# mLSTM attention with a feed-forward layer on one core: the later gates as 128 rows of chunk, sequence and head, and more bfloat16 products into tiles that are overwritten

## The chip, the core and the metric

The kernel runs on one core of a Trainium2 chip. The metric is device time in microseconds (us). A core has TensorE (PE, with its weight loads as PEld), VectorE (DVE), ScalarE (ACT), GpSimd (POOL) and SyncE (SP), which issues most of the DMAs here. Each engine carries out its instructions in the order of its own queue. An instruction that waits holds up everything behind it on its engine, and on no other.

## What is computed

Four sequences of eight heads have 768 tokens with 40 channels each. A gated recurrence (mLSTM) runs over the tokens, and its output is the input of a feed-forward layer with 2048 hidden units:

```
m_new = maximum(f_gate[t] + m, i_gate[t])
f_stab, i_stab = exp(f_gate[t] + m - m_new), exp(i_gate[t] - m_new)
C = f_stab * C + i_stab * outer(v[t], k[t])
n = f_stab * n + i_stab * k[t]
y[t] = sigmoid(o_gate[t]) * (C @ q[t]) / maximum(abs(n @ q[t]), 1)
...
h = x @ w_in                       # x: y as 3072 tokens of 320 channels
out = (maximum(h, 0) + alpha * minimum(h, 0)) @ w_out
```

## The kernel before

**Chunks.** Each sequence is cut into six chunks of 128 tokens, 24 in all. Inside a chunk the recurrence is an attention: scores pS = K Q, multiplied by a decay E = exp(L[t] + b[s]) that is zero for s > t, then times the values (pH). What came before the chunk enters through a state C, which `update` carries from chunk to chunk. L is the running sum, within a chunk, of lf = f + m(t-1) - m(t); b is i - m - L; the weights w = exp(b + L at the chunk's end), e = exp(L) and gam = exp(L at the chunk's end) scale the keys, the part from the state, and the state. The engines need b, w and e by token, as columns of bT, wT, eT, so they are transposed on PE. Two chunks make a group of 256 tokens; there are twelve groups, and the feed-forward layer runs group by group (`up`, `down`, lines 576 to 635) while the attention of the next group runs beside it.

**The gates.** They are kept as 32 rows (4 sequences x 8 heads, `BH`) of 768 tokens. `scan` (line 969) makes m for all tokens. Chunks 0 and 1 (columns `t0`) go first: lf0a, lf0b, li0, L0, bj0. Chunks 2 to 5 (columns `t1`, 512 of them) follow on POOL: lf1a and lf1b (lines 972 and 975), li1 (line 1037), then the running sum L1 on DVE (line 978), bj1 on POOL (line 1040), and after the written order `weights` (line 848), three Exp on ACT (lines 1099 to 1105), and twelve transposes of 32x128 by `by_token` (line 856). For chunks 2 and 3 L is spread over the partitions by a product with `pick` (line 412): LP holds three bfloat16 parts of L as 96 rows, so that one product adds all three. From chunk 4 on, L is read back from DRAM (`L_d`, written at line 1057) by a broadcast load Lb (line 113).

**The order.** The first group, up to its input x of the feed-forward layer, is written out as the string `ORDER` (line 559), and `pin` fixes it on every engine. Names in it: `dq0` and so on are DMAs on SP; `sp` spreads L, `ex` is the Exp of E, `ms` the mask of E on POOL (line 905), `sc` the scores, `wg` the product of both on DVE (line 925), `v0` and `v1` the values, `wd` the weighted keys kd (line 139), `w0s` to `w2l` the conversion of the first weights of the feed-forward layer, `x0` and `x1` the transposes of x (line 462). `warm12` is twelve bfloat16 products of the identity into a tile `junk` that nobody reads (line 942). After this string a scheduler lays out the rest; each engine takes it in that layout's order.

**Loads.** DMAs take eight semaphores in turn, over SP's and ACT's queues together, and each waits until the one before it on its semaphore has landed. SP's pinned order begins with f, q and k of chunks 0 and 1, weights, v, more weights (line 678) and the output gates `og` (line 122); the gates f and i come in by one load each (lines 817 and 818).

**After the string.** `weights(GC, NC)`, the conversion of two further weight blocks (w[3:]), the gates by token, gam, and `update(1)`; then FF0 and FF1 (the first two groups of the layer) with conversion of the other weights on ACT (lines 688, 710) and DVE (lines 700, 702, 714) beside the attention of chunks 2 to 5. From group 2 on the weights are there.

## Time and profile before

| | before |
|---|---|
| runs | 497.86, 503.60 and 499.66 us; median 499.66 us |
| the profiled execution | 500.96 us, its span 499.2 us |
| busy | PE 477.7 us (96%), DVE 321.6 (64%), ACT 321.6 (64%), POOL 304.8 (61%) |
| granted TensorE clock | 0.99 over the span |
| DMA | 61.60 MB |

The span is what the profiler's records cover; 1.76 us of the execution's time lie around it. Times in views are counted from the span's start. A row of the timeline has the start, the duration, the engine, the line, the operation with its tiles and its shape; in brackets at its end stands how long the engine idled before it, and what ended that. A row of the windows has a stretch, its length, the busy time of each engine in it, the granted clock and the share of time in which the 16 DMA engines had packets.

### The profile page before, as it was taken

To read this page: it belongs to the slowest core of one execution; us is meant where nothing else is said; L and a number is where in the kernel's file an instruction comes from. 1 tells how busy PE (TensorE), PEld (TensorE's weight loads), DVE (VectorE), ACT (ScalarE), POOL (GpSimd) and SP (SyncE) were. 2 spreads that over 40 slices of the span, in tenths; PEclk is the share of its full clock that TensorE was granted. 3 is DMA by queue.
4 is the path that set the end of the run, shared out by engine and by line. 5 is a ranking of instruction groups with operands and counts; after the bars stand their busy time and mean duration, and the time that the engine had idled before them with its cause. 6 is when DMAs were issued, how large, how long until landed. Compare 5 with 4: busy or idle time off the path is not lost.

```text
span 499.2 us, 11801 instructions
## 1 busy us (share of the span) xinstructions
PE 477.7 (96%) x4463; PEld 457.2 (92%) x4463; DVE 321.6 (64%) x676; ACT 321.6 (64%) x700; POOL 304.8 (61%) x393
## 2 busy tenths in 40 slices
PE   8889889989999999999899999999999999999997
PEld 7778879989989999989799999989999999999997
DVE  6889999934577686764395686567586575642321
ACT  3869697656587677756976677677886673343332
POOL 6632262306469889839498789858878755243242
PEclk9989997999999999999999999999999999999999
DMA  9999976345676566597557575769663130000000
GB/s 169 228 189 278 229 203 183 82 79 125 145 181 146 92 166 156 102 166 158 116 143 135 129 141 121 162 166 156 117 175 83 32 97 1 1 27 1 28 1 26
DMA packets 173922, 61.60 MB, mean 123 GB/s; under 512 B 140154, under 2 KB 166122, under 8 KB 173866
## 3 DMA queue, kind: packets, MB, share of 16 engines
q1 hardware_dynamic: 173786, 60.75, 55.3%
q8 instruction: 35, 0.57, 0.5%
q14 instruction: 21, 0.17, 0.1%
q10 hardware_dynamic: 80, 0.11, 0.1%
HBM read 36.90 MB, written 4.03 MB: 82 GB/s over the span
## 4 chain that ended last, share of the span: by engine, by line
PE 62%; DVE 8%; DMA 8%; ACT 8%; SPq 6%; issue 3%; POOL 3%; ACTq 0%; DVEq 0%; POOLq 0%
PE po L615 25%; PE ph L585 4%; PE ph L588 3%; PE ph L586 3%; PE ph L589 3%; PE ph L591 3%; PE ph L587 3%; PE ph L592 3%; PE ph L590 3%; DMA wo<-in_moe_w_out_dram 3%; PE pH L340 3%; PE pS L434 2%; SPq L678 2%; ACT E L418 2%; SPq L122 2%
## 5 line engine op out<-in xcount | busy, mean ns | idle before, releaser
L607 POOL TENSOR_TENSOR gl<-g,gh 128x512 fp32r<-128x512 f32 x80 | 102.9, 1287 | 62.2 <-ACT gh L606 55.0
L598 DVE SCALAR_TENSOR_TENSOR g<-g,oma,ph 128x256 f32<-128x256 f32 x160 | 69.8, 476 | 76.9 <-ACT g L594 73.1
L615 PE MATMUL po<-OH,gh 128*128 128x320 f32 x368 | 111.3, 314 | 0.0
L615 PE MATMUL po<-OL,gh 128*128 128x320 f32 x368 | 109.6, 311 | 0.0
L594 ACT ACTIVATE g<-ph 128x512 f32<-128x512 f32 x96 | 57.2, 596 | 43.7 <-PE ph L592 31.8
L615 PE MATMUL po<-OH,gl 128*128 128x320 f32 x368 | 71.9, 316 | 1.3 <-POOL gl L607 1.3
L606 ACT CAST gh<-g 128x512 fp32r<-128x512 f32 x80 | 49.5, 619 | 33.3 <-DVE g L598 32.0
L615 PEld LDWEIGHTS po<-OH,gh 128*128 128x128 f32 x368 | 69.0, 188 | 0.4 <-ACT gh L606 0.2
L615 PEld LDWEIGHTS po<-OL,gh 128*128 128x128 f32 x368 | 69.2, 188 | 0.2 <-DVE OL L714 0.2
L585 PE MATMUL ph<-XH,WH 128*128 128x256 f32 x192 | 58.5, 305 | 1.3 <-DVE g L598 0.9
L615 PEld LDWEIGHTS po<-OH,gl 128*128 128x128 f32 x368 | 56.9, 188 | 1.8 <-POOL gl L607 1.8
L418 ACT ACTIVATE E<-Lb,bT 128x128 f32<-128x128 f32 x160 | 50.9, 393 | 7.5 <-PE pH L340 7.2
L589 PE MATMUL ph<-X,W 128*128 128x256 f32 x192 | 55.2, 288 | 0.0
L586 PE MATMUL ph<-XH,WH 128*128 128x256 f32 x192 | 54.9, 286 | 0.0
L588 PE MATMUL ph<-XH,WL 128*128 128x256 f32 x192 | 54.6, 284 | 0.0
L591 PE MATMUL ph<-XL,WH 128*128 128x256 f32 x192 | 54.6, 284 | 0.0
L592 PE MATMUL ph<-X2L,W 128*128 128x256 f32 x192 | 54.5, 285 | 0.0
L587 PE MATMUL ph<-XH,WL 128*128 128x256 f32 x192 | 54.4, 284 | 0.0
L590 PE MATMUL ph<-XL,WH 128*128 128x256 f32 x192 | 54.2, 282 | 0.0
L422 POOL TENSOR_SCALAR_AFFINE_SELECT E<-E 128x512 f32<-128x512 f32 x44 | 30.0, 683 | 36.4 <-ACT E L418 36.4
L327 ACT CAST E<-pS 128x512 bf16<-128x512 f32 x72 | 41.8, 585 | 13.9 <-DVE pS L325 9.1
L585 PEld LDWEIGHTS ph<-XH,WH 128*128 128x128 f32 x192 | 36.6, 191 | 2.3 <-issue 1.1
(198 smaller groups left out, 1146.0 us busy)
## 6 DMA issues: line engine op xcount, KB each, us to landing
Lb<-L_d SPq DMA_DIRECT2D x20, 512.0 KB
wo<-in_moe_w_out_dram SPq DMA_DIRECT2D x8, 640.0 KB
wi<-in_moe_w_in_dram SPq DMA_DIRECT2D x8, 512.0 KB
qn<-in_q_dram SPq DMA_DIRECT2D x24, 160.0 KB
kn<-in_k_dram SPq DMA_DIRECT2D x24, 160.0 KB
va<-in_v_dram SPq DMA_DIRECT2D x24, 160.0 KB
og<-in_o_gate_dram SPq DMA_DIRECT2D x24, 160.0 KB
out_dram<-ob SPq DMA_DIRECT2D x11, 320.0 KB
```

Of the source, the lines that this page charges most:

```text
L418: nc.scalar.activation(E[:, p * P : (p + 1) * P], Lb[:, h] if Lb is not None else pb[:, p * P : (p + 1) * P], AF.Exp, bias=bT[:, c, b * H ...
L585: nc.tensor.matmul(dst, WH[half][:, 0, hs], XH[:, 0], start=True, stop=False)
L586: nc.tensor.matmul(dst, WH[half][:, 1, hs], XH[:, 1], start=False, stop=False)
L587: nc.tensor.matmul(dst, WL[half][:, 0, hs], XH[:, 0], start=False, stop=False)
L588: nc.tensor.matmul(dst, WL[half][:, 1, hs], XH[:, 1], start=False, stop=False)
L589: nc.tensor.matmul(dst, W2[:, fs], X2, start=False, stop=False)
L590: nc.tensor.matmul(dst, WH[half][:, 0, hs], XL[:, 0], start=False, stop=False)
L591: nc.tensor.matmul(dst, WH[half][:, 1, hs], XL[:, 1], start=False, stop=False)
L592: nc.tensor.matmul(dst, W2[:, fs], X2L, start=False, stop=True)
L598: nc.vector.scalar_tensor_tensor(out=y[:, e], in0=gt[:, e], scalar=oma[:, f : f + 1], in1=ph[:, e], op0=ALU.mult, op1=ALU.add)
L607: (nc.vector if g < 2 else nc.gpsimd).tensor_tensor(gl, y, gh.bitcast(F32), ALU.subtract)
L615: nc.tensor.matmul(po[j], x[:, e, j * P : (j + 1) * P], W[f // NB][:, f % NB], **ends)
```

## The change

**Gates of chunks 2 to 5.** They are laid out as 128 rows: chunk, sequence, head, each with its 128 tokens. f and i of these chunks are loaded once more for this, as four DMAs each of 32 rows of 128 tokens on ACT's queue, behind the loads of i and alpha. m, which is made as 32 rows, is copied to this layout by four DMAs from SBUF to SBUF on SP's queue (`m2d`). lf1a, lf1b, li1, bj1 on POOL and L1 on DVE then work on 128x128 instead of 32x512. The sum `weights` is gone for these chunks, since the Exp takes L at the chunk's end as its bias. Three transposes of 128x128 replace twelve. gam of chunks 2 to 5 and of chunk 1 are two small Exp, two DVE products with the identity and two PE products. L is written to `L_d` by five DMAs instead of one. LP holds its three parts side by side on 64 rows, so that the spread takes three products that accumulate, in place of one: 48 for 16; and one cast less makes LP.

**Products into overwritten tiles.** The order has `warm12` ahead of `u0m` and ahead of `x1`, 24 products more. `FILL` puts 4, 14 and 4 of them into the tile pH of chunks 3, 4 and 5, ahead of the products with the values, which overwrite it.

```diff
-    LP = const.tile([3 * BH, GT], BF16, tag="LP", name="LP")
-    pick = const.tile([3 * BH, BH], BF16, tag="pick", name="pick")
+    LP = const.tile([GC * BH, 3, P], BF16, tag="LP", name="LP")
+    pick = const.tile([GC * BH, GC * BH], BF16, tag="pick", name="pick")
...
+    def dense(dst, k):
+
+        x = ident.bitcast(BF16)
+        for _ in range(k):
+            nc.tensor.matmul(dst[:, : 2 * P], x[:, :P], x, start=True, stop=True)
...
     def values(n, E, busy=lambda: None):
 
         pH = psa(f"pH{n}")
+        dense(pH, FILL.get(n, 0))
...
-                    nc.tensor.matmul(
-                        pb[:, p * P : (p + 1) * P], pick[:, h : h + 1].broadcast_to([3 * BH, P]),
-                        LP[:, n % GC * P : (n % GC + 1) * P], start=True, stop=True,
-                    )
+                    x = n % GC * BH + h
+                    for k in range(3):
+                        nc.tensor.matmul(
+                            pb[:, p * P : (p + 1) * P], pick[:, x : x + 1].broadcast_to([GC * BH, P]), LP[:, k],
+                            start=k == 0, stop=k == 2,
+                        )
...
+    FILL = {3: 4, 4: 14, 5: 4}
...
+        def each_row(queue, dst, src, w=P):
+            for c in range(LC):
+                t = (GC + c) * P
+                queue.dma_start(dst[c * BH : (c + 1) * BH, :w], src[:, t : t + w])
...
+        each_row(nc.scalar, f2, f_gate.rearrange("b h s -> (b h) s"))
+        each_row(nc.scalar, i2, i_gate.rearrange("b h s -> (b h) s"))
...
+        def store_L():
+            nc.sync.dma_start(L_d[:, :GT], L[:, :GT])
+            for c in range(LC):
+                nc.sync.dma_start(L_d[:, (GC + c) * P : (GC + c + 1) * P], L2[c * BH : (c + 1) * BH])
...
-            lf1a=lambda: first_lf(1, t1, nc.gpsimd), lf1b=lambda: second_lf(1, u1, nc.gpsimd),
+            m2d=lambda: each_row(nc.sync, m2, m, P + 1),
+            lf1a=lambda: nc.gpsimd.tensor_tensor(l2, f2, m2[:, :P], ALU.add),
+            lf1b=lambda: nc.gpsimd.tensor_tensor(l2, l2, m2[:, 1:], ALU.subtract),
...
-            li1=lambda: nc.gpsimd.tensor_tensor(li[:, t1], i[:, t1], m[:, u1], ALU.subtract),
-            L0=lambda: sums(0, t0), L1=lambda: sums(1, t1),
+            li1=lambda: nc.gpsimd.tensor_tensor(b2, i2, m2[:, 1:], ALU.subtract),
+            L0=lambda: sums(0, t0),
+            L1=lambda: nc.vector.tensor_tensor_scan(L2, one2, l2, 0.0, ALU.mult, ALU.add),
...
-        weights(GC, NC, nc.gpsimd)
...
-        nc.scalar.activation(wj[:, GT:], wj[:, GT:], AF.Exp)
-        drain(by_token(bj, bT, "b", GC, GC, NC))
-        drain(by_token(wj, wT, "w", GC, GC, NC))
-        nc.scalar.activation(eL[:, GT:], L[:, GT:], AF.Exp)
-        drain(by_token(eL, eT, "e", GC, GC, NC))
...
+        nc.scalar.activation(w2, b2, AF.Exp, bias=L2[:, P - 1 :])
+        nc.scalar.activation(e2, L2, AF.Exp)
...
+        for src, dst in ((b2, bT), (w2, wT), (e2, eT)):
+            ps = psa("ps_g2")
+            nc.tensor.transpose(ps[:, :P], src, ident)
+            nc.vector.tensor_copy(dst[:, GC:].rearrange("p c a -> p (c a)"), ps[:, :P])
```

**Where the order stands now.** SP's queue in the pinned part, before (wi: weights, og: output gates, va: values, qn and kn: q and k):

```order
L678 DMA wi_1_179<-in_moe_w_in_dram 128x1024
L122 DMA og_181<-in_o_gate_dram 128x8x40 x2
L678 DMA wi_0_184<-in_moe_w_in_dram 128x1024
L122 DMA og_181<-in_o_gate_dram 128x8x40 x4
L106 DMA va_80<-in_v_dram 128x8x40 x2
L93 DMA qn_76<-in_q_dram 128x8x40
```

And changed:

```order
L688 DMA wi_1_188<-in_moe_w_in_dram 128x1024
L122 DMA og_190<-in_o_gate_dram 128x8x40 x2
L688 DMA wi_0_193<-in_moe_w_in_dram 128x1024
L122 DMA og_190<-in_o_gate_dram 128x8x40 x4
L835 DMA g_WL_95<-g_WL_95 32x129 x4
L106 DMA va_80<-in_v_dram 128x8x40 x2
```

The four copies of m stand behind all six loads of output gates and ahead of the next values.

POOL's queue in the pinned part, from the second mask of chunk 0 to the second of chunk 1, before:

```order
L905 AFFINE_SELECT E_1_265<-E_1_265 128x512
L972 TENSOR_TENSOR g_lf_139<-g_WH_94,g_WL_95 32x512
L975 TENSOR_TENSOR g_lf_139<-g_lf_139,g_WL_95 32x512
L905 AFFINE_SELECT E_0_302<-E_0_302 128x512
L1037 TENSOR_TENSOR g_li<-g_WH_94,g_WL_95 32x512
L139 TENSOR_TENSOR kd_383<-kn_78,wT 128x320
L905 AFFINE_SELECT E_1_316<-E_1_316 128x512
```

And changed:

```order
L928 AFFINE_SELECT E_1_278<-E_1_278 128x512
L1058 TENSOR_TENSOR g_WL_95<-g_WH_94,g_WL_95 128x128
L1059 TENSOR_TENSOR g_WL_95<-g_WL_95 128x128
L928 AFFINE_SELECT E_0_315<-E_0_315 128x512
L1061 TENSOR_TENSOR g_li<-g_WH_94,g_WL_95 128x128
L145 TENSOR_TENSOR kd_408<-kn_78,wT 128x320
L928 AFFINE_SELECT E_1_329<-E_1_329 128x512
```

The places are the same; the first of the 128x128 operations (lf1a) now reads what the copies of m bring. Behind it stand the two masks of chunk 1 (`ms10`, `ms11`) and its weighted keys.

DVE's queue around L1, before (t_wi and t_wr: weights in conversion):

```order
L700 TENSOR_SCALAR t_wi_1_326<-t_wi_1_326 128x512
L978 SCALAR_TENSOR_TENSOR g_L<-g_WL_95,g_lf_139 32x512
L700 TENSOR_SCALAR t_wr_344<-t_wr_344 128x512
L702 SCALAR_TENSOR_TENSOR t_wi_1_326<-wi_1_177,t_wi_1_326 128x512
L702 SCALAR_TENSOR_TENSOR t_wr_344<-wr_148,t_wr_344 128x512
L925 TENSOR_TENSOR E_0_302<-pS_0_374,E_0_302 128x512
```

And changed:

```order
L710 TENSOR_SCALAR t_wi_1_339<-t_wi_1_339 128x512
L1063 SCALAR_TENSOR_TENSOR g_L<-g_WL_95 128x128
L710 TENSOR_SCALAR t_wr_357<-t_wr_357 128x512
L712 SCALAR_TENSOR_TENSOR t_wi_1_339<-wi_1_186,t_wi_1_339 128x512
L712 SCALAR_TENSOR_TENSOR t_wr_357<-wr_157,t_wr_357 128x512
L948 TENSOR_TENSOR E_0_315<-pS_0_399,E_0_315 128x512
```

L1 keeps its place, between the steps of the weights' conversion and ahead of the products of scores and decays of chunk 1.

More of the change, by code (lines that the diff above doesn't have):

```diff
@@ L812, in chunks @@
             return x[:, c0 * P : c1 * P].rearrange("p (c t) -> p c t", t=P)
[L815 to L816 removed]
+        fi, rm = (const.tile([P, 2, DH], F32, tag=t, name=f"g_{t}") for t in ("WH1", "WL1"))
+        f, i, rst, m = fi[:BH, 0, :S], fi[:BH, 1, :S], rm[:BH, 0, :S], rm[:BH, 1, : S + 1]
+        LC = NC - GC
+        f2, i2, w2, e2 = fi[:, 0, S : S + P], fi[:, 0, S + P :], fi[:, 1, S : S + P], fi[:, 1, S + P :]
+        l2, one2, m2 = rm[:, 0, S : S + P], rm[:, 0, S + P :], rm[:, 1, S + 1 : S + P + 2]
+        def each_row(queue, dst, src, w=P):
+            for c in range(LC):
+                t = (GC + c) * P
+                queue.dma_start(dst[c * BH : (c + 1) * BH, :w], src[:, t : t + w])
         nc.sync.dma_start(f, f_gate.rearrange("b h s -> (b h) s"))
@@ L840, in first_group @@
             nc.vector.tensor_copy(row[j * BH : (j + 1) * BH], ident[j * BH : (j + 1) * BH, j * BH : (j + 1) * BH])
-        nc.vector.tensor_copy(pick, row.bitcast(F32))
-        li = row_tile("g_li", "Lb", bufs=2)
-        L = row_tile("g_L", "Lb", bufs=2)
+        nc.vector.tensor_copy(pick, ident[: GC * BH, : GC * BH])
+        both = [sb.tile([P, H, P], F32, tag="Lb", name=f"g_{x}", bufs=2).rearrange("p h t -> p (h t)") for x in ("li", "L")]
+        li, L = (x[:BH, :S] for x in both)
+        b2, L2 = (x[:, S : S + P] for x in both)
         bj, wj, eL = f, rst, i
@@ L935, in first_group @@
         junk = ps_o.tile([P, DM], F32, tag="o0", name="warm")
-        dense = ident.bitcast(mybir.dt.bfloat16)
         def warm(n=1):
-            for _ in range(n):
-                nc.tensor.matmul(junk[:, : 2 * P], dense[:, :P], dense, start=True, stop=True)
+            dense(junk, n)
         t0, u0 = slice(0, GT), slice(1, GT + 1)
```

52 lines of the change are left out of this document (26 added, 26 removed).

## The prediction, as it stood before the change was timed

> **What bounds the kernel now.** I read the windows by stretch first, with borders where the limit changes.
>
> ```profile
> core 0: us, PE busy (x) PEld busy (x) DVE busy (x) ACT busy (x) POOL busy (x), PEclk, DMA share, GB/s
> 0.00:26.00 26.00, 22.83 (x194) 19.66 (x195) 19.32 (x36) 15.62 (x35) 16.87 (x35) 1.00 1.04 198
> 26.00:31.00 5.00, 3.38 (x28) 2.50 (x25) 4.64 (x13) 1.15 (x3) 2.04 (x4) 1.00 1.45 155
> 31.00:41.00 10.00, 9.55 (x75) 8.39 (x74) 7.79 (x20) 8.63 (x15) 2.10 (x4) 0.83 0.70 228
> 41.00:62.00 21.00, 18.88 (x181) 17.66 (x182) 19.84 (x44) 16.26 (x36) 5.06 (x6) 1.00 1.01 251
> 62.00:97.00 35.00, 32.49 (x258) 31.12 (x258) 34.08 (x62) 28.86 (x69) 14.68 (x19) 0.90 0.59 156
> 97.00:110.00 13.00, 11.39 (x88) 11.13 (x86) 5.42 (x11) 6.47 (x9) 1.04 (x2) 1.00 0.58 117
> 110.00:499.20 389.20, 379.19 (x3648) 366.72 (x3648) 230.55 (x495) 244.62 (x537) 262.99 (x327) 1.00 0.49 106
> ```
>
> From 110 us on PE is busy 97% of the time at full clock; the change leaves that stretch as it is, and only moves its start. From 62 to 97 us DVE is the limit (34.08 of 35 us), from 41 to 62 us DVE (19.84 of 21) beside DMA engines that never rest (1.01). Ahead of that the DMAs are saturated too, and DVE has gaps: 0.36, 2.21, 1.16 and 0.92 us in the four stretches from 26 to 97 us, 4.65 us in all. Whatever makes DVE late at 26 us is therefore late at 97 us, less what these gaps give back. The chain of waits goes on from there to PE:
>
> ```profile
> 102.77 3.37 DMA og<-in_o_gate_dram
> ```
>
> The output gates of the second sequence can be loaded only once chunk 5 has used those of the first; ACT waits for them, and PE for ACT:
>
> ```profile
> 109.92 0.41 PE L615 MATMUL po<-OH,gg 128*128 128x320 f32 x1 [1.61 <-ACT gg L606]
> ```
>
> So a late DVE is a late start of the stretch that PE bounds.
>
> **Copies of m: when they land.** SP's own queue in the timeline:
>
> ```profile
> 17.96 4.39 SPq L122 DMA_DIRECT2D og<-in_o_gate_dram  x4
> 22.39 1.59 SPq L106 DMA_DIRECT2D va<-in_v_dram  x2
> 24.11 0.59 SPq L93 DMA_DIRECT2D qn<-in_q_dram  x1
> ```
>
> The sixth output gate is issued at 22.35 us, since SP waits for room in a saturated DMA. The four copies stand right behind. At 0.6 us each (qn's issue) the last goes out at 24.2 us. How long it needs is bounded by two rows: the load of i, on DMAs almost empty, was issued at 0.80 us, and DVE's scan, which waits for it, starts at 4.14:
>
> ```profile
> 0.80 0.43 ACTq L818 DMA_DIRECT2D g_WH<-in_i_gate_dram  x1
> ```
>
> ```profile
> 4.14 1.75 DVE L969 TENSOR_TENSOR_SCAN g_WL<-g_WH 32x768 f32<-32x768 f32 x1 [1.16 <-DMA g_WH<-in_i_gate_dram]
> ```
>
> 3.3 us from issue; the values of the loaded queue give 3.79 us more after 0.7 us of issue, in the chain of waits:
>
> ```profile
> 23.16 3.79 DMA va<-in_v_dram
> ```
>
> The copies are small (32 rows of 516 bytes), so I take the short one and a little less, 3.1 us: landed at 27.3 us. Bounds: 26.0 us if issues take 0.43 us and the rest 2.2 (an estimate, two thirds of i's), 29 us if the eight additional loads push the output gates by 1 us and the copies take va's time.
>
> **What waits for them.** lf1a on POOL, at 14.50 us before:
>
> ```profile
> 8.43 0.60 POOL L848 TENSOR_TENSOR g_WL<-g_WH,g_L 32x256 f32<-32x256 f32 x1 [1.14 <-DVE g_WH L1039]
> ...
> 14.50 1.26 POOL L972 TENSOR_TENSOR g_lf<-g_WH,g_WL 32x512 f32<-32x512 f32 x1
> 15.83 1.15 POOL L975 TENSOR_TENSOR g_lf<-g_lf,g_WL 32x512 f32<-32x512 f32 x1
> 16.95 0.62 POOL L905 TENSOR_SCALAR_AFFINE_SELECT E<-E 128x512 f32<-128x512 f32 x1
> 17.55 1.08 POOL L1037 TENSOR_TENSOR g_li<-g_WH,g_WL 32x512 f32<-32x512 f32 x1
> 18.60 0.96 POOL L139 TENSOR_TENSOR kd<-kn,wT 128x320 f32<-128x320 f32 x1
> ```
>
> Behind it on POOL are both masks of chunk 1, and its result is what DVE's L1 waits for. An operation of 128 columns has no row; 0.60 us for 256 and 1.15 for 512 bound it between nothing and 0.60, and I take 0.45. So lf1a and lf1b end at 28.2 us, the first mask at 28.8, li1 and kd at 30.3, the second mask at 30.9. On DVE:
>
> ```profile
> 7.00 0.83 DVE L978 TENSOR_TENSOR_SCAN g_L<-g_WL,g_lf 32x256 f32<-32x256 f32 x1
> ...
> 15.96 3.02 DVE L139 TENSOR_TENSOR kd<-kn,wT 128x320 f32<-128x320 f32 x1
> ...
> 21.87 1.21 DVE L978 TENSOR_TENSOR_SCAN g_L<-g_WL,g_lf 32x512 f32<-32x512 f32 x1
> 23.00 0.39 DVE L700 TENSOR_SCALAR t_wr<-t_wr 128x512 uint32<-128x512 uint32 x1
> ...
> 25.65 0.68 DVE L925 TENSOR_TENSOR E<-pS,E 128x512 f32<-128x512 f32 x1
> ```
>
> L1 began at 21.87 us and begins at 28.2, 6.3 us later. It then has 128 columns: 0.83 us for 256 and 1.21 for 512 give 0.6, so 0.6 us come back. The rest up to the second product of chunk 1 is the same 3.3 us (23.00 to 26.33) and covers the masks. kd, 3.02 us beside a busy POOL, may take less beside a waiting one, but that only lengthens DVE's wait. **Term one: +5.7 us**, with the bounds of landing and POOL +4.2 to +7.5.
>
> ACT is also later. Its last load of i waits, by the turns of the semaphores, for a load that itself waits for i, so two landings of 3.3 us lie ahead of it, and it goes out at some 7.5 us with the table load behind it. Before, ACT was ready 3.56 us ahead of its first copy, at 3.0 us:
>
> ```profile
> 6.57 0.58 ACT L874 COPY qf<-pqk 104x512 f32<-104x512 f32 x1 [3.56 <-PE pqk L218]
> ```
>
> That makes its copies up to 3 us later and the first Exp less than that. The wait at L1 covers it at no cost; without that cover it would be up to +3 us. The values, q and k of the next chunks, behind the copies on SP, go out 2.4 us later, which FF0's first products cover, since these come later by as much.
>
> **What comes back after 31 us.** POOL's sum of 32x512 is gone, the Exp shrink from 512 to 128 columns, nine small transposes are gone; L's writes go from one to five issues on SP, ahead of weights whose staging waits for a late DVE anyway. None of this is DVE work, so it can only close DVE's gaps: 2.21 us from 31 to 41 us, at most 3.73 us up to 62. In the same stretch PE had a clock of 0.83, after pauses like the second here:
>
> ```profile
> 24.46 1.04 PE L942 MATMUL warm<-ident 128*128 128x256 bf16 x8
> ...
> 28.89 0.60 PE L942 MATMUL warm<-ident 128*128 128x256 bf16 x4
> 30.62 0.41 PE L462 MATMUL p<-ident,xn 128*128 128x128 f32 x2 [1.14 <-DVE xn L394]
> ```
>
> A clock of 0.83 over 10 us is 1.7 us lost. Twelve products at 0.11 us (eight take 1.04, four 0.60) are 1.3 us, which fills the 1.14 us ahead of x1. If they keep the clock, FF0 feeds DVE 1.7 us sooner. **Term two: -1.7 us**, nearer to the gaps of 31 to 41 us than to nothing, bounds -3.7 to 0.
>
> The Trainium skill, "TensorE: Matmul & The Clock Gate" (What's actually happening), has the clock fall only after an idle window of about 3.4 us. The rows show the clock down after single pauses of 1.14 us and less, so here the row decides; by the rule the filler would keep nothing, and with nothing in place of term two the sum below would end 1.7 us higher.
>
> **More work on PE.** The spread:
>
> ```profile
> 42.78 0.38 PE L412 MATMUL pb<-LP,pick 96*128 96x128 bf16 x4
> ```
>
> Four take 0.38 us, so one adds at most 0.095 us and 32 more at most 3.0 us, since the end of one overlaps the next; PE's 2.1 us idle of 41 to 62 us, where DVE is the limit, hide them; without that cover they cost up to 3.0 us. The fills of chunks 3 and 4 (18 products, 2.0 us) lie in the 2.5 us that PE idles from 62 to 97; the four of chunk 5 come when PE hardly rests. **Term three: +0.4 us**, bounds 0 to +5. Keeping the clock there (0.90, after waits for DVE as in
>
> ```profile
> 72.81 2.98 PE L304 MATMUL pH<-va,E 128*128 128x42 f32 x16 [1.48 <-DVE E L440]
> ```
>
> ) makes PE faster where DVE is the limit. I take nothing; at most 10% of 35 us, -3.5 us.
>
> **Sum.** 5.7 - 1.7 + 0.4 = +4.4 us on the profiled execution's 500.96 us: 505.4 us. That execution lies 1.3 us over the median of the runs, 499.66; the forecast for a median is 504.1 us.
>
> **Rivals.**
>
> *Absorbed.* The wait is there, but POOL's and ACT's shorter queues let DVE close all its gaps up to 62 us, and a PE at full clock in 62 to 97 us is worth half its bound: 5.7 - 3.7 - 1.8 = +0.2, so 499.9 us. For it: 3.7 us of gaps. Against: 34.08 of 35 us busy behind them.
>
> *No wait (the other side).* SP reaches the copies so early that they land before DVE comes to L1. That needs them landed by 20.9 us (21.87 less two POOL operations), issued by 17.6, ahead of the output gates' last four. Then terms two and the shorter scan remain, and the clock of 62 to 97 at half: -1.7 - 0.6 - 1.8 = -4.1, with all of it -5.8: 494 to 496 us. Against: SP issues in order, and DMA at 1.04 sets its pace.
>
> *Cold start.* PE, done with chunk 1's scores, idles for the 5.7 us of the wait and comes back at half clock. The sixteen products ahead of x1 then take 3.4 us in place of 1.8, x1 is 1.6 us late, and term two vanishes: 5.7 + 1.6 + 0.4 = +7.7, 507.4 us. For it: the half clock after much shorter pauses. It decides if the clock is low when x1 is due. The Trainium skill's rule (same page and section) speaks for this one, since such a wait is longer than its window.
>
> **Chances.** Forecast 0.40 (501 to 506 us), absorbed 0.25, no wait 0.10, cold start 0.25. A measurement of this kernel tells about 1% (5 us) from no change: faster 0.09 (most of no wait, little of absorbed), same 0.53 (most of absorbed, two thirds of the forecast), slower 0.38 (cold start and the forecast's upper third). The range, 497 to 509 us, leaves out no wait and the upper bounds of both terms.
>
> **What would show it.** Right: POOL idles from about 15.5 us to 27 before lf1a, released by a DMA; DVE idles some 6 us before L1; ph of FF0 starts at 36 to 38 us; at 62 to 97 us nothing shrinks; PE's last wait for ACT's gg comes 3 to 6 us later. Term two: clock near 1.0 in the stretch of FF0's first ph. Wrong: lf1a before 22 us, or DVE at 97 us as early as before although lf1a was late.

## The result and the profile after

The changed kernel takes 515.74 us (median of 511.77 to 517.17) beside 500.61 us for the kernel before, a ratio of 1.0275 [1.0231, 1.032]: slower, and 6.7 us above the upper end of the predicted range. The profiled execution took 515.52 us with a span of 513.8, 14.6 more than before. The windows of the changed kernel, with the prediction's borders:

```profile
core 0: us, PE busy (x) PEld busy (x) DVE busy (x) ACT busy (x) POOL busy (x), PEclk, DMA share, GB/s
0.00:26.00 26.00, 23.10 (x128) 18.89 (x129) 10.30 (x25) 11.27 (x28) 8.29 (x28) 0.74 0.98 193
26.00:31.00 5.00, 5.00 (x57) 4.59 (x55) 3.72 (x7) 3.05 (x5) 3.89 (x7) 0.98 0.68 112
31.00:41.00 10.00, 9.23 (x80) 8.09 (x80) 8.79 (x22) 4.09 (x9) 3.25 (x5) 1.00 0.75 160
41.00:62.00 21.00, 16.78 (x139) 14.81 (x137) 17.08 (x37) 15.49 (x34) 5.16 (x5) 0.76 0.81 208
62.00:97.00 35.00, 34.05 (x307) 32.04 (x306) 31.65 (x62) 28.39 (x65) 10.46 (x14) 1.00 0.66 176
97.00:110.00 13.00, 11.82 (x109) 11.44 (x108) 12.24 (x26) 8.00 (x18) 4.94 (x7) 1.00 0.44 124
110.00:513.80 403.80, 388.89 (x3727) 376.33 (x3726) 234.88 (x502) 251.73 (x544) 263.76 (x329) 1.00 0.51 105
```

Before, the clock was 1.00 in the first stretch and is now 0.74; it was 0.83 at 31 to 41 us and is 1.00; it was 1.00 at 41 to 62 us and is 0.76. DVE was the limit from 41 to 97 us and no longer is.

**The start, 7.6 us.** Two things are late here, at the same place. The first is ACT. Its timeline begins with DMA issues (ACTq is its queue of them):

```profile
1.73 3.22 ACTq L835 DMA_DIRECT2D g_WH<-in_f_gate_dram  x4
5.95 3.23 ACTq L835 DMA_DIRECT2D g_WH<-in_i_gate_dram  x4
9.21 1.28 ACT L897 ACT_TABLE_LOAD   x1 [9.21 <-DMA g_WH<-in_f_gate_dram]
10.50 0.59 ACT L897 COPY qf<-pqk 104x512 f32<-104x512 f32 x1
```

The eight added loads hold ACT until 9.21 us, and its first copy comes at 10.50 in place of 6.57. PE waits for it, once, and from 12.6 us on, 1.4 us after it is back at work, its clock is at half until 26.2 us. The same engine's rows, of the changed kernel:

```profile
11.14 0.23 PE L1007 MATMUL pa<-ident,al 16*128 16x16 f32 x1 [1.47 <-ACT qf L897]
...
23.48 3.26 PE L137 MATMUL warm<-ident 128*128 128x256 bf16 x16
26.67 0.51 PE L167 MATMUL pu<-va,kd 128*40 128x42 f32 x16
```

and where that last product stood before:

```profile
19.08 0.51 PE L161 MATMUL pu<-va,kd 128*40 128x42 f32 x16 [1.74 <-ACT kf L270]
```

It is 7.6 us late. In the kernel before PE had paused too, for 1.74 us, and its clock stayed at 1.00, so the length of a pause alone does not decide what it costs. Sixteen products take 3.26 us here; twelve of them are the added `warm12`. The second thing is the one that was predicted, the copies of m, on SP and then on POOL:

```profile
22.56 2.50 SPq L835 DMA_DIRECT2D g_WL<-g_WL  x4
```

```profile
26.34 0.41 POOL L1058 TENSOR_TENSOR g_WL<-g_WH,g_WL 128x128 f32<-128x128 f32 x1 [8.48 <-DMA g_WL<-g_WL]
```

They land at 26.3 us (predicted 27.3), and an operation of 128 columns takes 0.41 us (predicted 0.45). DVE's own row shows that the other cause came last:

```profile
27.23 0.68 DVE L182 COPY C<-pu 40x168 f32<-40x168 f32 x2 [5.89 <-PE pu L167]
...
29.54 0.85 DVE L1063 TENSOR_TENSOR_SCAN g_L<-g_WL 128x128 f32<-128x128 f32 x1
```

DVE's wait is for PE, not for POOL; by then m is there. L1 starts at 29.54 us in place of 21.87, and the second product of chunk 1 ends at 33.90 in place of 26.33.

**The middle, 4.8 us.** PE reaches the spread and runs dry behind it:

```profile
47.64 0.84 PE L421 MATMUL pb<-LP,pick 64*128 64x128 bf16 x12
...
52.07 2.07 PE L447 MATMUL pS<-qf,kf 104*128 104x128 f32 x8 [3.01 <-DVE C L187]
...
54.92 1.46 PE L421 MATMUL pb<-LP,pick 64*128 64x128 bf16 x12
```

The clock is down again, to half from 50.1 to 60.4 us: twelve spread products take 0.84 us ahead of the pause and 1.46 behind it. What PE waits for is an addition to the state C on DVE. In this kernel's order it stands behind a step in the conversion of an output weight (t_wo), DVE waits there for ACT, and ACT for the load of that weight (wo):

```profile
50.12 0.77 ACT L698 ACTIVATE t_wo<-wo 128x640 f32<-128x640 f32 x1 [1.95 <-DMA wo<-in_moe_w_out_dram]
```

```profile
50.93 0.49 DVE L710 TENSOR_SCALAR t_wo<-t_wo 128x640 uint32<-128x640 uint32 x1 [1.79 <-ACT t_wo L698]
51.34 0.68 DVE L187 TENSOR_TENSOR C<-C,pu 40x168 f32<-40x168 f32 x2
```

In the order of the kernel before, the addition stood ahead of that step:

```profile
42.88 0.67 DVE L181 TENSOR_TENSOR C<-C,pu 40x168 f32<-40x168 f32 x2
43.59 0.49 DVE L700 TENSOR_SCALAR t_wo<-t_wo 128x640 uint32<-128x640 uint32 x1
```

PE's last wait for ACT's gg, which the prediction used to mark the start of the late stretch, has moved from 109.92 us by 12.35:

```profile
122.27 0.42 PE L625 MATMUL po<-OH,gg 128*128 128x320 f32 x1 [2.07 <-ACT gg L616]
```

**The rest, 2.2 us.** From that row to the end of the span are 391.5 us; before, from 109.92 to 499.2, 389.3.

### The profile page after: what moved, and what is told of

The parts are those of the page before. It is cut to its first block, busy times and chain, and to the rows that moved or that the text cites. A ratio compares the mean times of both kernels' runs of the same rounds, so it can differ in the third digit from the quotient of the medians.

```text
span 513.8 us, 11962 instructions
## 1 busy us (share of the span) xinstructions
PE 488.9 (95%) x4534; PEld 466.2 (91%) x4534; DVE 318.7 (62%) x677; ACT 322.0 (63%) x700; POOL 299.8 (58%) x393
## 4 chain that ended last, share of the span: by engine, by line
PE 67%; DMA 13%; ACT 6%; POOL 4%; DVE 3%; issue 2%; SPq 2%; ACTq 0%; POOLq 0%; DVEq 0%
PE po L625 26%; DMA kS<-Z 4%; PE ph L595 4%; PE ph L601 3%; PE ph L598 3%; PE ph L596 3%; PE ph L599 3%; PE ph L597 3%; PE ph L602 3%; PE ph L600 3%; DMA qS<-Z 3%; PE pH L347 2%; PE pS L443 2%; DMA wo<-in_moe_w_out_dram 2%; ACT E L427 1%
## 5 line engine op out<-in xcount | busy, mean ns | idle before, releaser
L599 PE MATMUL ph<-X,W 128*128 128x256 f32 x192 | 54.6, 285 | 0.3 <-DVE W L724 0.3
L596 PE MATMUL ph<-XH,WH 128*128 128x256 f32 x192 | 54.6, 284 | 0.0
L334 ACT CAST E<-pS 128x512 bf16<-128x512 f32 x72 | 41.9, 586 | 12.6 <-DVE pS L332 8.7
```

Of the source, the lines that this page charges most:

```text
L596: nc.tensor.matmul(dst, WH[half][:, 1, hs], XH[:, 1], start=False, stop=False)
L599: nc.tensor.matmul(dst, W2[:, fs], X2, start=False, stop=False)
```

## The experiments

The gates' own edits (rows, loads, copies, spread) and the 46 products were taken apart. Ratios are to the kernel before in the same job. Where the text does not say that an order was kept, the scheduler laid out the program anew, and the two runs compared differ in their order as well. By the traces e2 has the changed kernel's order on PE, DVE, ACT and POOL, and e3, e9 and e11 share one. The order of e1 leaves that of the changed kernel, and of e11, at some 58 us; e4, e7 and e8 leave that of the kernel before, and e5 that of e3, between 37 and 41 us. Further below, another order alone is worth between nothing and nearly 1%.

| run | what it is | median us | ratio, 95% |
|---|---|---|---|
| e1_two_loads | changed kernel, two loads for eight | 516.31 | 1.0271 [1.0214, 1.0328] |
| e2_copies_early | changed kernel, copies of m early | 510.82 | 1.0136 [1.0072, 1.0201] |
| e3_both | both of these | 511.85 | 1.0188 [1.0126, 1.025] |
| e4_before_act_loads | before, with the eight loads | 507.37 | 1.0112 [1.0075, 1.0149] |
| e5_both_no_fills | e3 without the 46 products | 507.30 | 1.009 [1.0057, 1.0123] |
| e6_both_one_product | e5 with one spread product for three | 510.75 | 1.0146 [1.0074, 1.0218] |
| e7_before_fills | before, with the 46 products | 498.49 | 0.9914 [0.9875, 0.9953] |
| e8_before_x1 | before, with the twelve ahead of x1 | 499.98 | 0.9956 [0.9915, 0.9996] |
| e9_copies_mid | e3, copies behind two weight blocks | 511.37 | 1.0152 [1.0087, 1.0216] |
| e10_before_fills_three | e7 with three spread products | 504.71 | 1.0047 [1.0009, 1.0084] |
| e11_no_copies | e3 without any copy of m | 508.60 | 1.0113 [1.0078, 1.0147] |
| e12_three_laid_as_one | e10 in the order of e7 | 503.91 | 1.0042 [1.001, 1.0075] |
| e13_one_laid_as_three | e7 in the order of e10 | 498.55 | 0.9918 [0.9883, 0.9952] |
| e14_gates_one_laid_as_three | e6 in the order of e5 | 507.09 | 1.0094 [1.0058, 1.0131] |
| e15_gates_three_laid_as_one | e5 in the order of e6 | 511.57 | 1.0185 [1.0142, 1.0227] |
| e16_one_plain | e7, plain DMAs for transposing ones | 493.54 | 0.982 [0.9781, 0.9858] |
| e17_three_plain | e12, the same | 497.35 | 0.9898 [0.9859, 0.9938] |
| e18_gates_plain | e11, the same | 497.29 | 0.9896 [0.9849, 0.9944] |

### The two late starts

Theory A: the eight loads on ACT cool PE. Theory B: the late copies of m make DVE wait.

```diff
-        each_row(nc.scalar, f2, f_gate.rearrange("b h s -> (b h) s"))
-        each_row(nc.scalar, i2, i_gate.rearrange("b h s -> (b h) s"))
+        for dst, src in ((f2, f_gate), (i2, i_gate)):
+            nc.scalar.dma_start(dst, src.rearrange("b h s -> (b h) s")[:, GT:].rearrange("a (c t) -> c a t", t=P))
```

> f and i of chunks 2 to 5 come by one load each on ACT's queue instead of four, so that ACT waits for no landing there. Theory A (the eight loads hold ACT until 9.2 us, PE cools and the start runs at half clock): ACT copies q at 6.6 us again instead of 10.5, the clock from 10 to 26 us is 1.0 instead of 0.5 to 0.63, and only the copies of m are left to wait for, so DVE ends the second product of chunk 1 at 31 to 32 us instead of 33.9 (26.3 before); 513 us. Theory B (the late copies of m alone make the loss): no change, 515.7 us. If the copies do not count at all: 26.5 us there and 508 us.

It took 516.31 us, as long as with eight loads. ACT's first copy is back at 6.62 us, and POOL and DVE now show the wait that was predicted:

```profile
27.75 0.41 POOL L1058 TENSOR_TENSOR g_WL<-g_WH,g_WL 128x128 f32<-128x128 f32 x1 [12.52 <-DMA g_WL<-g_WL]
```

```profile
28.68 0.83 DVE L1063 TENSOR_TENSOR_SCAN g_L<-g_WL 128x128 f32<-128x128 f32 x1 [5.89 <-POOL g_WL L1059]
```

The second product of chunk 1 ends at 33.90 us again. The windows of this run show what the wait does to PE, which has nothing else to do:

```profile
26.00:31.00 5.00, 0.00 (x0) 0.00 (x0) 2.32 (x3) 0.30 (x1) 3.17 (x6) 0.83 0.65 105
31.00:41.00 10.00, 8.06 (x46) 7.24 (x47) 7.44 (x17) 2.08 (x6) 3.65 (x6) 0.57 0.77 166
```

So B alone costs what A and B cost together, as far as the other order of e1 behind 58 us leaves that open. That both kernels end the second product at 33.90 us is chance: in the changed kernel DVE waited for PE, which was behind ACT, and here for POOL, which was behind the copies.

```diff
-    ORDER = """dq0 dq1 dw0 dw2 warm24 dv0 dw1 dw4 do1 dw3 do2 scan lf0a ... kT0 kc0 m2d warm12 sp00
+    ORDER = """dq0 dq1 dw0 dw2 warm24 dv0 scan m2d dw1 dw4 do1 dw3 do2 lf0a ... kT0 kc0 warm12 sp00
```

> The four copies of m stand ahead of the second weights and the output gates on SP, the eight loads stay on ACT. Theory A: lf1a on POOL comes early, but DVE's second product of chunk 1 still ends at 33 to 34 us, since PE is cold; 515 us, within 1.5 us. Theory B: it ends at 28 to 29 us; 510 us.

510.82 us: B's number, in the same order on all engines but SP, so the place of the copies is worth 1.4%, 7 us. DVE's second product ends at 28.84 us, as B has it. But B is not all of it: PE waits for ACT's late copy here too (1.01 us), and this time the clock is at half only from 11.4 to 14.8 us. Had it stayed low as long as in the changed kernel, PE would presumably have held DVE up again. Why it came back sooner is not shown, and the mean clock of a kernel's runs varies (0.973 to 0.983 in the four of the changed kernel). The next has both edits.

> Both edits at once. Theories A and B together: no wait at the start is left, the second product of chunk 1 ends at 26 us as before. If the further 5 us that the change loses between 34 and 122 us follow from being late, 499 to 501 us; if they come from the new order of products and the spread by three, 504 to 506 us. If neither theory holds: above 510 us.

511.85 us, the case in which neither theory holds. The front is still 3 us late, since the copies now hold SP, and a weight block behind them is late for ACT:

```profile
9.65 7.04 SPq L835 DMA_DIRECT2D g_WL<-g_WL  x4
```

```profile
21.06 0.67 ACT L698 ACTIVATE t_wi<-wi 128x512 f32<-128x512 f32 x1 [2.44 <-DMA wi<-in_moe_w_in_dram]
```

Theory A by itself, on the kernel before (the eight loads go to tiles that nobody reads):

```diff
+        each_row(nc.scalar, f2, f_gate.rearrange("b h s -> (b h) s"))
+        each_row(nc.scalar, i2, i_gate.rearrange("b h s -> (b h) s"))
```

> The kernel before, with the eight loads of f and i on ACT's queue, whose data nobody reads. Theory A: ACT copies q at 10.5 us instead of 6.6, half clock from 13 us on, 4 to 8 us slower than before, 505 to 508 us. Theory B: 500 to 502 us.

507.37 us: the loads alone cost 1.1%, 5.6 us, where no other wait covers them, with what the new order behind 37 us adds or takes.

Since e3 left some 11 us unexplained, the copies were moved again, and then left out. All engines but SP and, in the second, the operands of three POOL operations keep e3's order.

```diff
-    ORDER = """dq0 dq1 dw0 dw2 warm24 dv0 scan m2d dw1 dw4 do1 dw3 do2 lf0a
+    ORDER = """dq0 dq1 dw0 dw2 warm24 dv0 dw1 dw4 do1 scan m2d dw3 do2 lf0a
```

> Both starts mended once more, but the four copies of m stand on SP behind the two weight blocks that chunk 1's conversions need and ahead of the next one; PE, DVE, ACT and POOL have the same order as with the copies early (511.85 us), SP differs in the place of the copies alone. There the copies held SP from 9.65 to 16.73 us, and ACT's next conversion waited for a weight block, so DVE's second product ended at 29.38 us in place of 26.33. Theory C (the rest of the loss is what the copies hold on SP): second product by 27 us, 505 us or less. Theory O (the rest is the layout of the middle): the front comes 2 to 3 us sooner, 508 to 510 us, and PE still waits 2 us and more for DVE's C ahead of pS.

```diff
-            lf1a=lambda: nc.gpsimd.tensor_tensor(l2, f2, m2[:, :P], ALU.add),
-            lf1b=lambda: nc.gpsimd.tensor_tensor(l2, l2, m2[:, 1:], ALU.subtract),
+            lf1a=lambda: nc.gpsimd.tensor_tensor(l2, f2, f2, ALU.subtract),
+            lf1b=lambda: nc.gpsimd.tensor_tensor(l2, l2, l2, ALU.subtract),
...
-            li1=lambda: nc.gpsimd.tensor_tensor(b2, i2, m2[:, 1:], ALU.subtract),
+            li1=lambda: nc.gpsimd.tensor_tensor(b2, i2, f2, ALU.subtract),
```

> The one before without the copies at all: lf1a, lf1b and li1 take f and i in place of m, so the gates of chunks 2 to 5 leave m out. The order of the other engines is the same once more. Theory C: 499 to 503 us, no slower than the kernel before by more than 0.5%, since nothing is late. Theory O: 505 to 509 us. If it comes to 497 to 499 us, as the kernel before with the same 46 products did, the layout of gates on 128 rows costs nothing and the copies are all of the loss.

With the copies in the middle it is 511.37 us, since SP is held there too:

```profile
17.27 4.05 SPq L835 DMA_DIRECT2D g_WL<-g_WL  x4
```

Without copies it is 508.6 us. There the front is that of the kernel before (chunk 1's second product begins at 25.91 us, before at 25.65), and 1.1% stays. So the copies cost 1.6% where the change put them (e1 against e11, which also differ in order), 0.4 to 0.8% elsewhere (the intervals of these two overlap with e11's), and the gates have another cost that is not at the start. Its place can be read in e11's trace: PE has the same pause ahead of pS as in the changed kernel, for the same reason (DVE's conversion step waits 2.00 us for ACT, and the addition to C behind it), and the clock is at half from 44.3 to 54.6 us:

```profile
44.95 2.07 PE L447 MATMUL pS<-qf,kf 104*128 104x128 f32 x8 [3.22 <-DVE C L187]
```

So the pause of the middle comes without any late start. No run has this order with the addition alone moved.

### The products

```diff
-        u0m qc1 u0c v0
+        warm12 u0m qc1 u0c v0
...
-        x0 warm4 tadd g1r g1g s0a w2h g1x g1p w2l x1
+        x0 warm4 tadd g1r g1g s0a w2h g1x g1p w2l warm12 x1
...
         pH = psa(f"pH{n}")
+        x = ident.bitcast(BF16)
+        for _ in range({3: 4, 4: 14, 5: 4}.get(n, 0)):
+            nc.tensor.matmul(pH[:, : 2 * P], x[:, :P], x, start=True, stop=True)
```

> The kernel before and all 46 added products, and nothing else of the change. Theory P: 503 to 506 us (5.5 us of products, less what lies in waits of 1 to 2 us). Theory O: 499 to 502 us. The prediction had 24 of them worth -1.7 us and the fills at +0.4: 499.3 us.

> The kernel before and only the twelve products ahead of x1: term two of the prediction by itself, whose DVE is not late. If the clock of 0.83 from 31 to 41 us goes to 1.00 and DVE's gaps close by as much, as the prediction had it: 498 to 499.5 us. If DVE and the DMAs set the pace there whatever PE's clock is: 500 to 502 us.

On the kernel before, all 46 give 0.9914, the twelve ahead of x1 0.9956: they gain about 4 and 2 us, each in an order of its own (e13 below has 0.9918 with the 46 in another). Theory P, that they are PE time which nothing hides, is wrong, and the prediction's term two (-1.7 us) was about right. e7 is also faster than both kernels, and no other version that leaves nothing out beats it clearly.

> The changed kernel with both starts mended (two loads on ACT, copies of m early) and without any of its 46 added bfloat16 products; the gates as 128 rows and the spread with three products stay. With the products it took 511.85 us, some 11 us over the kernel before. Theory P (the products are PE time that nothing hides: sixteen took 1.91 us at full clock, so 46 are 5.5 us): 505 to 508 us. Theory O (what is left is the layout of the middle, where PE waits 2.8 us for DVE's C ahead of pS with no product of the feed-forward layer to do, and comes back at half clock): 510 to 513 us, with a granted clock of 0.8 or less from 41 to 62 us.

e5 is e3 without them: `FILL = {}`, and both added `warm12` gone. 1.009 against 1.0188: on the gates as rows no gain from the same products is to be seen. What they do there the pair does not tell, since e5's order differs too: in it the addition to C (47.55 us) stands ahead of the conversion step (48.91 us) again, and PE waits for it 0.21 us in place of 3. Next, e5's spread with one of its three products, `for k in range(1)`:

> The one before, and the spread takes only its first product of three, so that L is spread as one bfloat16 part (two of the three parts are left out). Twelve took 0.84 us at full clock and 1.46 at half. Theory P: 32 products fewer at 0.06 us, 2 us less than the one before. Theory O: either nothing, if the wait for C stays where it is, or 3 us and more, if the layout then puts products of the feed-forward layer ahead of pS.

1.0146, slower with less to do, though its interval reaches into e5's. The scheduler had laid out the program anew: of the instructions after the written order, hundreds stand in other places once a step's length changes. Work and order had to be separated.

### Three spread products for one: the work or the order

On the kernel before with its 46 products:

```diff
-                    nc.tensor.matmul(
-                        pb[:, p * P : (p + 1) * P], pick[:, h : h + 1].broadcast_to([3 * BH, P]),
-                        LP[:, n % GC * P : (n % GC + 1) * P], start=True, stop=True,
-                    )
+                    for _ in range(3):
+                        nc.tensor.matmul(
+                            pb[:, p * P : (p + 1) * P], pick[:, h : h + 1].broadcast_to([3 * BH, P]),
+                            LP[:, n % GC * P : (n % GC + 1) * P], start=True, stop=True,
+                        )
```

> The kernel before with the 46 added products (498.49 us) and its spread product issued three times, each overwriting the one before it, so that 48 stand for 16; gates and copies as before. Term three of the prediction (hidden in waits for DVE): 498.5 to 499.5 us. If the longer spread puts off the scores and DVE behind them, as it seems to where PE waits for C: 501 to 504 us.

1.0047 against 0.9914: 1.3%, 6.7 us, for 32 products that the prediction put at 0.4. For the next four the program is laid out twice: once with the number of products that is to set the order, of which only the order is kept, and once with the number that is to run, each engine fixed to that order:

```diff
+    order = build(..., 1, None)
+    nc = build(..., 3, order)
...
+            for k in order:
+                for i in ahead.get(k, []) + [by_key[k]]:
+                    if i.engine in last:
+                        tc.add_manual_dep(i, last[i.engine].name, ..., reason="order")
+                    last[i.engine] = i
```

> The kernel before with the 46 added products and three spread products for one (1.0047 of before in the scheduler's own layout), but every engine's instructions in the order that the scheduler laid out for one product (0.9914 of before); only the 32 products more stand between. Theory S (the 32 products cost it themselves: PE time, scores later): ratio 1.002 to 1.007, 502 to 504 us on a before of 501. Theory O (the products cost at most their 2 us, and the rest of the 6.5 us is that a longer spread makes the scheduler lay out the rest of the program in another order): ratio 0.990 to 0.996, 496 to 499 us.

> The reverse: one spread product, in the order that the scheduler laid out for three. Theory S: ratio 0.989 to 0.994, as the kernel before with the 46 products. Theory O: ratio 1.000 to 1.005, 501 to 503.5 us, with the waits that the three products had in their own layout (values vb on POOL 0.96 us, the reciprocal's r on DVE 1.35, gh on ACT 1.36).

The two runs fall on theory S: three products in the order of one take 1.0042, one in the order of three 0.9918. The order is not it; the 32 products are, at three times their own length. On the gates as rows it is the other way round:

> The gates as 128 rows with both starts mended and no added products, the spread cut to one of its three products (two parts of L left out), in the order laid out for three (1.009 of before with three, while one product in its own layout took 1.0146). Theory S: the ratio of one product, 1.012 to 1.017, cannot come from products that are fewer, so it has no account of this pair and expects 1.004 to 1.009. Theory O: 1.005 to 1.010, since the order is that of the faster layout.

> The same gates with all three products, in the order laid out for one. Theory O: 1.0146 and up to 2 us of products more, ratio 1.013 to 1.019. If orders matter little: 1.009 as in its own layout, within 0.4%.

There one product and three take the same in the order laid out for three (1.0094 and 1.009), and both are slower in the order laid out for one (1.0146 and 1.0185; clear of noise for three products only). So either can cost half a per cent and more, and neither is a price per product; on the gates the 32 products cost nothing in one order and 0.4%, within noise, in the other.

### Where 32 products cost 6 us

e7 and e12 have the same order, and nothing is late at 110 us. PE's row at gg, of e7, then of e12:

```profile
109.29 0.41 PE L618 MATMUL po<-OH,gg 128*128 128x320 f32 x1 [0.41 <-ACT gg L609]
```

```profile
109.73 0.42 PE L622 MATMUL po<-OH,gg 128*128 128x320 f32 x1 [1.12 <-ACT gg L613]
```

From there to the end of the span e7 needs 385.8 us (span 495.1) and e12 390.8 (span 500.5): 5.0 of the 5.4 us are made where no product was added. A piece of that stretch in e12:

```profile
268.13 0.46 ACT L231 CAST Z<-qn 128x320 bf16<-128x320 f32 x1 [4.93 <-DMA kS<-Z]
...
269.48 0.87 DVE L605 SCALAR_TENSOR_TENSOR g<-g,oma,ph 128x256 f32<-128x256 f32 x2 [5.54 <-ACT g L601]
...
270.50 0.35 PE L592 MATMUL ph<-XH,WH 128*128 128x256 f32 x1 [1.02 <-DVE g L605]
```

ACT casts q into a tile Z, from which a transposing DMA makes the operands of the later chunks' scores. The tile is free once the transposing DMA of an earlier chunk has read it. ACT waits for that, the layer's activation g stands behind, DVE waits for g, and PE for DVE. These waits of ACT summed (total us, times, longest), from 110 to 480 us, in e7 and then in e12:

```profile
ACT Z L230 <- DMA kS<-Z: 15.8, 8, 3.5
...
ACT Z L230 <- DMA qS<-Z: 2.2, 2, 1.3
```

```profile
ACT Z L231 <- DMA kS<-Z: 18.1, 7, 4.9
...
ACT Z L231 <- DMA qS<-Z: 4.1, 3, 1.7
```

18.0 us against 22.2. In the changed kernel, whose stretch took 391.5 us, it is 24.8:

```profile
ACT Z L236 <- DMA kS<-Z: 20.0, 8, 4.9
ACT Z L236 <- DMA qS<-Z: 4.8, 3, 2.3
```

But the sums do not follow the length of the stretch everywhere. In e11, where it is 393.3 us long (below), they come to 20.8:

```profile
ACT Z L236 <- DMA kS<-Z: 15.2, 6, 4.5
...
ACT Z L236 <- DMA qS<-Z: 5.6, 3, 2.6
```

Theory T: the extra is made in these waits. To try it, the transposing DMAs became plain ones of the same tiles, in the same orders, so the transposition is left out:

```diff
-            nc.sync.dma_start_transpose(X[:, 1], Z[:, j].rearrange("p h x -> p (h x)"))
+            nc.sync.dma_start(X[:, 1], Z[:, j])
```

> The kernel before with the 46 products (0.9914), in the same order, with the 36 transposing DMAs of the later chunks' q and k as plain DMAs of the same tiles (the transposition is left out, so the scores of chunks from 12 to 23 are of other numbers). It is the base for the next two. If the transposing DMAs and ACT's waits for them hold up the late stretch: 0.980 to 0.990. If PE alone sets its pace: 0.990 to 0.993.

> The same with three spread products for one, in the same order. With transposing DMAs the three cost 1.28% (1.0042 against 0.9914), although the products lie at 43 to 76 us and DVE was not late at 62 to 97 us; ACT's waits for the transposing DMAs grew from 18.0 to 22.3 us in all. Theory T (the extra is made in these waits): 0 to 0.5% over the one before, that is at most the products' own 2 us. Theory S (the 32 products cost it in another way): 1.0 to 1.5% over it.

> The gates as 128 rows with two loads, no copies, all added products and three spread products (1.0113), in their own order, with plain DMAs for transposing ones. Theory T: 0 to 0.7% over the kernel before with plain DMAs and one spread product. Theory S, or a cause in the layout of the gates that has nothing to do with these DMAs: 1.5 to 2.3% over it, as with transposing ones.

The base is 0.982, faster still. Three products cost 0.8% over it (1.3% with transposing DMAs), between what the two theories said; the gates with three products and no copies 0.8% (2.0%), just above theory T's bound. The second fall, from 2.0 to 0.8%, is clear of the intervals; the first, from 1.3 to 0.8%, is not. The stretch from gg to the end can be compared in the profiled executions. PE's row there in e16, e17 and e18:

```profile
110.72 0.42 PE L625 MATMUL po<-OH,gg 128*128 128x320 f32 x1 [0.81 <-ACT gg L616]
```

```profile
112.11 0.39 PE L625 MATMUL po<-OH,gg 128*128 128x320 f32 x1
```

```profile
113.76 0.41 PE L631 MATMUL po<-OH,gg 128*128 128x320 f32 x1 [1.65 <-ACT gg L622]
```

and in e11, the gates with transposing DMAs:

```profile
113.69 0.41 PE L625 MATMUL po<-OH,gg 128*128 128x320 f32 x1 [1.84 <-ACT gg L616]
```

| gg to the end, us | one product | three | gates, three |
|---|---|---|---|
| transposing DMAs (e7, e12, e11) | 385.8 | 390.8 | 393.3 |
| plain DMAs (e16, e17, e18; spans 492.0, 495.8, 495.2) | 381.3 | 383.7 | 381.4 |

In each column the order is the same above and below. With plain DMAs the late stretch differs by 2.4 us at most; with transposing ones by 5.0 and 7.5. So in these executions about half of what the 32 products cost behind gg, and nearly all that the gates cost there, goes with these DMAs. Each length is of one execution, and the runs of one kernel lie up to 5.3 us apart (e12). It is also not shown that ACT's waits are the way. They are not gone with plain DMAs (13.3 us in e17 against 3.6 in e16, whose stretches differ by 2.4), and the swap changes more than them: a transposing DMA from Z to kS holds SP for 1273 ns (median, e7), a plain one for 536 (e16), and the busy share of the DMA engines falls from 55.3 to 49.3%. In e11 the clock is also at half twice in this stretch (157 to 160 us and 341 to 345 us), in e7, e12 and the three with plain DMAs never; of its 7.5 us that can be 3.4. Ahead of gg e17 is 1.4 us later than e16, and e18 3.0; e18 has PE's pause for C again (3.24 us). In e17 this comes with a lower clock, which was not tested by itself; the window from 76 to 90 us of e16, then of e17:

```profile
76.00:90.00 14.00, 13.39 (x107) 12.93 (x105) 13.51 (x27) 9.94 (x21) 3.97 (x4) 0.96 0.53 164
```

```profile
76.00:90.00 14.00, 13.94 (x83) 13.75 (x83) 11.94 (x25) 9.06 (x20) 3.19 (x4) 0.70 0.56 170
```

Not settled is why 0.44 us of lateness at 110 us grows to 5.4 in an order that is the same: in e12 the waits at these DMAs come out longer one after the other, but which transfer each of them meets was not followed. One more Z tile, which would spare ACT the wait and keep the transposition, was not tried.

## Why the prediction was wrong, point by point

In steps from run to run, the ratio goes from 1 to 0.9914 (46 products), 1.0047 (three spread products), 1.0113 (gates as rows, no copies), 1.0271 (copies where they were put) and 1.0275 (eight loads for two): -4, +7, +3, +8 and 0 us of some 501. The third step's intervals just overlap; the others, but for the last, are apart. The steps are not prices that can be moved about: each also changes the order of the program. The second was measured without that, too: 6.4 us on the kernel before (e12 against e7), but nothing or 2 us on the gates as rows (e14 against e5, e6 against e15).

By stretches of the two profiled executions the forecast was +5.7 us at the start, -1.3 in the middle (terms two and three) and nothing behind 110 us; measured were 7.6, 4.8 and 2.2. So the largest miss, 6 us, is in the middle.

- **Copies of m land at 27.3 us; POOL and DVE wait.** Right: 26.3 us, 0.41 us an operation, L1 at 28.68 in e1, where nothing else is late (predicted 28.2). Term one, +5.7 us, measured 7.0 by the changed kernel against e2, whose order is the same (the clock has its part in this), and 7.9 by e1 against e11, whose order is not. It was short by what the cold start rival adds: in e1 PE does nothing from 26 to 31 us and has a clock of 0.57 behind it. In the changed kernel itself this wait was not the last to end.
- **ACT up to 3 us later, covered at no cost.** In the sum it came out so (e1 takes what the changed kernel takes, in another order), but by luck. ACT is 3.9 us late, half clock follows PE's 1.47 us of waiting for it, and PE is 7.6 us late at its update, so that the start is late by ACT's loads, with the wait for m under their cover. Without the cover they cost 5.6 us (e4), not 3.
- **Term two, -1.7 us.** About right on the kernel before: 0.9956 [0.9915, 0.9996], some -2.2 us, with another order behind 37 us. The clock of FF0's stretch went to 1.00 in the changed kernel as well. But there nothing of it is left at 110 us, since the pause of the middle comes behind it.
- **"None of this is DVE work, so it can only close DVE's gaps."** This step failed, with the largest miss. What changed was the order behind the pinned part: DVE's addition to C came to stand behind a conversion step that waits for ACT and for a load, PE waited 3.01 us for it, and its clock was at half from 50.1 to 60.4 us. The stretch lost 4.8 us where 1.3 were to be gained. The same pause in e11 (3.22 us) and e18 (3.24), where the start is not late, shows that it does not come from the late start, and in e5, with the gates as rows too but in another order, PE waits 0.21 us there; e11 comes to gg 4.0 us later than e12 (113.69 against 109.73 us), in whose order the addition stands first. That the pause makes up these 4.0 us is read from the traces and was not tried by itself.
- **Term three, +0.4 us, bounds 0 to +5.** This step failed too, on the kernel before. The fills were no cost (e7), but the 32 spread products cost 6.7 us on the kernel before (e10) and 6.4 in an unchanged order (e12 against e7). Their own 2 us are hidden ahead of 110 us, as predicted; what follows from them is not. What they cost in the changed kernel is open, since on the gates as rows they cost between nothing and 2 us.
- **"From 110 on PE is busy 97% of the time at full clock; the change leaves that stretch as it is, and only moves its start."** This is the assumption behind it, and it failed. PE's share of 97% hid chains such as the one through ACT and the transposing DMAs, which set PE's pauses there; the stretch took 389.3 us before, 391.5 in the changed kernel, and from 385.8 (e7) to 393.3 us (e11) in others with transposing DMAs. A profile's share of busy time says that little is to be gained on the other engines, not that nothing can be lost.
- **At 62 to 97 us nothing shrinks, DVE stays the limit.** Wrong for the changed kernel: DVE has 31.65 of 35 us busy and PE 34.05. That FF0's products came late to DVE after the pause at 52.07 us fits this and was not followed further.

Of the rivals, cold start (507.4 us) came nearest, and its mechanism is there: in the changed kernel not in the wait for m but behind ACT's late copy, and again from 50.1 us on. The Trainium skill, "TensorE: Matmul & The Clock Gate" (What's actually happening), speaks of an idle window of about 3.4 us; here the clock is down after one pause of 1.47 us, with PE busy on both sides of it, so the trace goes on differing, as the prediction held. But the prediction's own reading, that single pauses of 1.14 us and less bring the clock down, is no rule either: the pause of 1.74 us in the kernel before did not. The Trainium skill, "Advanced Engine Details and Errata" (X-Bar Transpose (TRN2)), states that transposing DMAs are as fast as regular ones. How long one transfer takes was not measured here; one holds SP for 1273 ns against 536 for a plain one, and putting plain ones in their place takes the ratio from 0.9914 to 0.982.

## What to carry to other kernels

Before a stretch is called bound by one engine and only moved, look at who releases that engine's few remaining pauses: if it is a chain through a DMA, its length can change with what comes in, by more than the work that was added. Where a scheduler lays out what follows the part that is written by hand, read the order that it makes after the change, too: here one step that waits for a load, put ahead of an addition that PE needs, came with a pause of 3 us and 10 us at half clock. A set of small copies holds the engine whose queue issues it: four of 32 rows held SP for 2.5 to 7 us and ACT's eight loads held ACT for 6.5, and whatever stands behind them must be able to wait. Before a difference is put down to the work or to the order, fix the order and change the work, and then the reverse.

## What the hardware did that was not expected

- The weighted keys kd on DVE took 0.49 us in the changed kernel, with POOL idle, where they had taken 3.02 beside a busy POOL; the row of the timeline:

```profile
20.25 0.49 DVE L145 TENSOR_TENSOR kd<-kn,wT 128x320 f32<-128x320 f32 x1
```

- One pause of 1.47 us on PE, with work before and behind it, was followed from 12.6 to 26.2 us by a clock of 0.50; the windows of 10 to 25 us of the changed kernel:

```profile
10.00:20.00 10.00, 8.86 (x46) 7.29 (x46) 3.20 (x11) 5.43 (x15) 1.27 (x2) 0.63 1.07 233
20.00:25.00 5.00, 5.00 (x26) 4.36 (x26) 1.34 (x4) 4.08 (x12) 0.00 (x0) 0.50 0.90 190
```

PE was busy for 13.86 of these 15 us, so being busy did not bring the clock back at once. The pause of 1.74 us in the kernel before was followed by a clock of 1.00 up to 31 us, and e2's of 1.01 us for the same copy by 0.50 from 11.4 to 14.8 us only. What sets how long it stays low is not shown.
